# Attention with relative bias and a gated MLP on one core: softmax transposed in 32x32 blocks, and the value product in eight small tiles

## The chip, the core and the metric

The kernel runs on one core of a Trainium2 chip. A core has five engines with a queue each: TensorE (PE, matrix products into PSUM; weight loads are listed apart as PEld), VectorE (DVE), ScalarE (ACT), GpSimd (POOL) and SyncE (SP), which here only issues DMA transfers. The metric is the device time of one execution in microseconds (us); lower is better.

## What is computed

Eight batches, eight heads, 576 positions, head width 64: attention with a bias that a small network makes from the relative position, then a causal five-tap convolution that gates a linear layer, then a second linear layer. All in f32.

```python
scores = scale * np.matmul(q, k.transpose(0, 1, 3, 2))
x = (psi_rel / psi_i)[..., None]
h = np.maximum(x @ w1 + b1, 0.0)
bias = h @ w2
scores = scores + bias.transpose(2, 0, 1)[None, :, :, :]
attn = np.exp(scores - max); attn = attn / (sum + 1e-09)
x = np.matmul(attn, v)                      # then heads side by side: 512 columns
gate_pre += conv_w[k] * xp[:, k:k + S, :]   # k = 0..4
out = (1 / (1 + np.exp(-gate_pre))) * (x @ w_val) @ w_out
```

## The kernel before

**Order.** The Python code does not issue instructions at once. Each step is added to a planner (`Plan.add`) with the engines that may do it, a price on each, the steps it depends on, a priority and the buffers it takes. `Plan.order` simulates the engines with these prices and emits the steps in the order that it finds; on each engine they then run strictly in that order, and wait for one another by semaphores. `OFFS`, `PAIR_AT`, `MLP_AT`, `LOOK` and `LOAD` are tuned numbers of that planner, `BUFS` the number of buffers of each ring: `sp` are score buffers of two PSUM banks, `ps` single PSUM banks, `e` SBUF tiles for exponentials, `pt` tiles for transposed ones.

**Stages.** First the bias for all heads is made in 36 row groups (L338 to L380) and stored to DRAM. Then 32 pairs follow. A pair is one batch `b`, one half of the heads `hg` and one `l`: two heads, stacked on the upper and the lower 64 partitions. `RUNS` gives the order of the pairs; the bias tiles of a half of the heads stay in SBUF during a run and are loaded again at the next (`load_bias`). When all four pairs of a batch are done, its `mlp` may start.

**A pair.** The 576 queries are four chunks of 128 and a last one of 64. For each chunk: scores of both heads (`qkm`, L617), two 64-row tiles of PE side by side; logits with the row minimum (`logits`, DVE, L659); exponential with row sum (`expo`, ACT, L671). For the last 64 queries both heads share one tile, one head above the other, over 640 columns padded with a large negative bias (L629). Then the weights must be transposed so that keys lie on partitions. `TRANS` chooses one of two ways for each pair:
- "T" (13 pairs): the weights are scaled (`norm`, L716), transposed on PE (`tp`, L756) into PSUM, copied out (`tev`), and multiplied with V in f32 (`piece`, L826).
- "D" (19 pairs): the weights are split into two f16 parts (`top`, `rest`, L247, L254), transposed by DMA (`swap`), and multiplied with V, which is split and transposed too (L559 to L575), in three f16 products. The scaling follows at the end: reciprocals are transposed (L876), spread over rows (`rb`, L883) and multiplied in (`mu`, L887).

The last 64 queries have their own value product (`rem_mm`, L902). The result goes straight into the batch's tile `xp` in the batch's second run; in its first run it is stored to DRAM (`store`) and loaded again (`ldx`).

**The MLP.** In seven batches the convolution runs through PSUM in halves of 288 columns (`taps`, L1009 and L1016, all but the first tap on DVE). In the last batch `conv`, `prod` and `acc` do it in SBUF (L966 to L981) on three engines. The products with `w_val` (`val`, L1073) and `w_out` (`outp`, L1130) take three passes each with operands split in two parts.

Of the kernel before, what the change touches and what calls it, by code (L numbers as in the profile page):

```python
# [10 lines left out]
F16 = mybir.dt.float16  # L11
# [21 lines left out]
NEG = -1.0e30  # L33
RW = S + REM
# [4 lines left out]
RUNS = ((0, (0, 1, 2, 3)), (1, (0, 4, 1, 5, 2, 6, 3)), (0, (4, 5, 6, 7)), (1, (7,)))  # L39
MLP_STEPS = 32  # L40
MLP_AT = (28, 16, 18, 8, 12, 10, 17, 38)
PAIR_AT = (-0.5, -1, -2.5, -0.5, -2, 1, 2.5, -2, -2.5, -2.5, 2.5, -1.5, -1.5, -2, 2.5, -1.5, 1.5, -2.5, 0, 2, 1.5, 1.5, -2.5, -0.5, -3.5, -5, -7.5, -7.5, 0, -0.5, 0.5, 1.5)
TRANS = tuple(x == "T" for x in "TTTTDTTTTTTDDTDDDDDTDTDDDDDDDDDD")
BUFS = dict(w=13, d=5, pt=2, sp=2, ps=4, qk=3, rel=4, be=6, xp=2, xh=1, gh=1, gx=1, rt=2)
RING = dict(er="w", hlr="w", raw="w", e="d", hl="d", xo="w", vt="w", ptr="w", gate="w", gf="w", ot="w", tt="ps", po="ps", pm="ps", cv="ps")
LOOK = dict(w=20.89, ps=50.18, d=6.14, be=3.54, gh=38.67, pt=1.31, xh=172.47, sp=0.72, xp=0.18)
DRAIN = 0.07
# [3 lines left out]
    "conv acc relu norm rest top split_hi split_lo glo ghi vlo double_step w_sub w_lo cw".split()  # L51
)
MODES = dict(qkm=1, piece=2, rem_mm=2, bias_mm=3, rb=4)
SMALL = (("G", 0.19), ("V", 0.08))
LOAD = dict(P=0.95, V=1.2, A=0.36, G=0.47, S=0.08)
OFFS = dict(ldx=1, swap=4, qk_ld=1.75, qkm=-5, norm=4, piece=4, val=0.75, outp=7.25, mur=3.25, bias_store=2.5, conv=-1.75, taps=-2.25, split_hi=0.25, rb=-7.5, rest=-9.25, rev=-10, ldv=0.5, w_hi=8, logits=1.75, relu=0, ost=1.25, bias_fin=1.5, ote=-2.5, double_step=5.25, store=4.75, ghi=1, sig=3, vtr=1.25, recip=-4.25, glo=-2.75, ev=-1.5, tev=4.25, evr=3.5, w_sub=-1.75, gf=0.5, w_ld=-1.25, mu=-1, w_lo=7.5, bias_mm=0.5, bias_ld=1.5, expo=0.75, rtp=-0.25, prod=5.25, vlo=3.25, cw=2, vhi=3.25, eps=-2.25, vmax=-6.25, acc=-0.25, split_lo=2, close_bias=1.5, rem_mm=0, top=0.75, vinv=-0.25, tp=-6.25)
# [19 lines left out]
class Plan:  # L76
# [10 lines left out]
    def add(self, engines, fn, deps=(), pri=0.0, takes=(), uses=(), hold=0.5, wire=0.0):  # L87
        pri += OFFS.get(getattr(fn, "func", fn).__name__, 0.0)
        t = Task(engines, fn, [d for d in deps if d is not None], pri, list(takes))
        t.pri = max([pri] + [d.pri for d in t.deps])  # L90
        t.n, t.hold, t.wire = len(self.tasks), hold, wire
        name = getattr(fn, "func", fn).__name__
        t.shares = "GV" if name in SHARED else "G"
        t.mode = MODES.get(name, 0)
        for b in uses:
            b.users.append(t)
        self.tasks.append(t)
        return t

    def order(self):  # L100
# [30 lines left out]
        while ready:  # L131
# [28 lines left out]
            e = min(pick, key=lambda e: pick[e][1])  # L160
# [6 lines left out]
            else:  # L167
                if e == "P":
# [4 lines left out]
                    cost = cost * (2 if slow else 1) + 0.012 + DRAIN * (t.mode != mode)  # L173
# [32 lines left out]
def attention_gated_mlp(  # L206
# [3 lines left out]
    vd: bass.AP,  # L210
    vn: bass.AP,
# [5 lines left out]
    identd: bass.AP,  # L217
    seld: bass.AP,
# [12 lines left out]
    for k in set(BUFS) & {"sp", "ps", "w", "d", "pt", "qk"}:  # L231
# [85 lines left out]
    def bias_rows(m):  # L317
# [10 lines left out]
        pbs = [Buf("tt") for _ in pieces]  # L328
# [20 lines left out]
        for g in range(4):  # L349
            eng = [("A", 0.22 + 0.54 * w / S)] if g == 0 else [("V", 0.1 + 0.4 * w / S), ("G", 0.15 + 2.6 * w / S)]  # L350
# [4 lines left out]
        def bias_mm(e, j):  # L355
            pb = bank(pbs[j])
            x, y = pieces[j]
            for g in range(4):
                T.matmul(
                    pb[32 * g : 32 * g + 32, 0 : y - x],  # L360
# [7 lines left out]
        def bias_fin(e, j, lo, hi, back):  # L368
# [3 lines left out]
            i = pbs[j].t[:, lo - x : hi - x]  # L372
# [10 lines left out]
        first = None  # L383
        for j, (x, y) in enumerate(pieces):
            t = add([("P", 0.1 + 0.5 * (y - x) / HS)], partial(bias_mm, j=j), rts, pri + 0.3, [pbs[j]], [rel[0]])
            for back, n, l in ((False, wf, fs), (True, wb, bs)):
                lo, hi = max(x, 1 if back else 0), min(y, n)
                if lo >= hi:
# [7 lines left out]
                    [pbs[j]],  # L396
# [27 lines left out]
    def load_bias(run, hg, l, c, pri):  # L424
# [3 lines left out]
        def bias_ld(e):  # L428
            if c < NM:
                SP.dma_start(biasm[l][c], bias_rows_of(c, 2 * p, 2))  # L430
            else:
                SP.dma_start(biasr[l][0:REM, 0:S], bias_rows_of(c, 2 * p, 1))
                SP.dma_start(biasr[l][REM:P, REM:RW], bias_rows_of(c, 2 * p + 1, 1))

# [50 lines left out]
    def weight(src, n, hi_lo, k, last, pri):  # L485
        b = {}

        def w_ld(e):
            b["r"] = pools["mp"].tile([P, 1024], I32, name="wraw", tag="xp0")[:, 0 : 2 * n]
# [34 lines left out]
    spilled, arrived, taker = {}, {}, {}  # L524

    def pair(n):
        hg, b, l = order[n]
        p = 2 * hg + l
        run = sum(1 for x in range(1, n + 1) if order[x][0] != order[x - 1][0])
        s0 = PER * n + PAIR_AT[n]  # L530
        tr = TRANS[n % len(TRANS)]
        top_, bot = slice(0, D), slice(D, P)

        qk = Buf("qk")

        def qk_ld(e):
            SP.dma_start(new(qk, [P, S + RW], F32), qkd[b, p])

        loaded = add([("S", 1.73)], qk_ld, (), s0 - 8, [qk])
        vt = Buf("vt")  # L540
        sc = {}
        if tr:

            def ldv(e):
                new(vt, [P, 5, P], F32)
                SP.dma_start(vt.t.rearrange("p t d -> p (t d)"), vn[b, p])

            tv = add([("S", 0.9)], ldv, (), s0 - 1, [vt])
        else:
            vhl, raw = Buf("raw"), Buf("raw")  # L550

            def ldv(e):
                new(vhl, [P, 2, RW], F16)
                new(raw, [P, RW], F32)
                SP.dma_start(raw.t, vd[b, p])

            def vmax(e):
                sc["t"] = smp.tile([P, 4], F32, name="vsc", tag="vsc", bufs=5)
                V.tensor_reduce(out=sc["t"][:, 0:1], in_=raw.t, op=ALU.max, axis=AX.X, apply_absolute_value=True)  # L559

            def vscale(e):
                t = sc["t"]
                (V if e == "V" else G).tensor_scalar(
                    out=t[:, 1:2], in0=t[:, 0:1], scalar1=1e-30, scalar2=2.0**-12, op0=ALU.max, op1=ALU.mult
                )

            def vinv(e):
                t = sc["t"]
                V.reciprocal(out=t[:, 2:3], in_=t[:, 1:2])

            def vhi(e):
                A.activation(out=vhl.t[:, 0, :], in_=raw.t, func=AF.Copy, scale=sc["t"][:, 2:3])

            def vlo(e):
                V.scalar_tensor_tensor(  # L575
# [654 lines left out]
```

## Time and profile before

| | before |
|---|---|
| median of 2 runs | 764.64 us (762.93 to 766.36) |
| span of the profiled execution | 759.0 us |
| instructions | 17283 |
| largest queue | q1: 258420 packets, 133.95 MB |

The page gives the span of the profiled execution, from its first to its last instruction; its own device time isn't listed beside it. The median of the runs is 5.64 us above the span. The busy share of an engine is the time in which at least one of its instructions runs. In a group's row stand line, engine, operation, output<-inputs, shapes and count, then the busy time of the group, the mean of one instruction in ns, and the idle time just before them with what ended it. An f32 matmul leaves two records.

### The profile page before, as it was taken

How to read it: one execution, taken by the hardware profiler on the slowest of the kernel's cores; microseconds unless marked ns; L12 is line 12 of the kernel's file. 1: busy time of each engine (PE TensorE's matmuls, PEld its weight loads, DVE VectorE, ACT ScalarE, POOL GpSimd, SP SyncE). 2: the span in 40 equal slices, each digit the busy share in tenths (PEclk: the TensorE clock that was granted, in tenths of full speed). 3: DMA queues.
4: the chain of work that ended last, by engine and by line, in shares of the span. 5: the costliest groups of instructions: out<-in, count | busy, mean ns of one | idle time of the engine just before them, and what ended most of it. 6: DMA issues, size and time to landing. Idle time of an engine off the chain costs nothing.

```text
span 759.0 us, 17283 instructions
## 1 busy us (share of the span) xinstructions
PE 716.5 (94%) x6091; PEld 485.7 (64%) x6091; DVE 587.5 (77%) x1606; ACT 580.8 (77%) x1302; POOL 476.1 (63%) x550
## 2 busy tenths in 40 slices
PE   5577999999999999999899999999999999999997
PEld 2124666665566666767566677666767786767886
DVE  6996878777789897886759778869998878856830
ACT  6996788767578897889767876789797967797642
POOL 0002467765455685777975494859797587768852
PEclk9999999999999999999999999999999999999999
DMA  8898442968332878899999599599999999999702
GB/s 293 284 287 287 134 119 69 223 198 260 127 111 82 165 157 200 175 196 186 221 207 197 162 243 274 119 221 214 212 175 222 218 265 243 255 193 187 134 29 70
DMA packets 263754, 144.48 MB, mean 190 GB/s; under 512 B 231538, under 2 KB 231796, under 8 KB 263668
## 3 DMA queue, kind: packets, MB, share of 16 engines
q1 hardware_dynamic: 258420, 133.95, 76.7%
q10 hardware_dynamic: 5248, 9.44, 3.9%
q8 instruction: 48, 0.79, 0.4%
q14 instruction: 38, 0.31, 0.1%
HBM read 61.03 MB, written 25.05 MB: 113 GB/s over the span
## 4 chain that ended last, share of the span: by engine, by line
PE 50%; POOL 3%; DMA 3%; DVE 3%; ACT 2%; issue 1%; SPq 0%; POOLq 0%; DVEq 0%; ACTq 0%
PE t_ps L1073 12%; PE t_ps L1130 11%; PE t_sp L617 10%; PE t_ps L826 9%; DMA t_pt<-t_d 3%; PE t_sp L629 2%; PE t_ps L883 2%; PE t_ps L756 2%; POOL t_d L254 2%; PE t_ps L902 2%; PE t_ps L876 1%; DVE t_d L659 1%; ACT t_d L671 1%; DVE xl L254 0%; POOL xl L254 0%
## 5 line engine op out<-in xcount | busy, mean ns | idle before, releaser
L671 ACT ACTIVATE t_d<-t_d,nm 128x576 f32<-128x576 f32 x256 | 197.9, 774 | 67.7 <-DVE nm L659 67.0
L254 POOL TENSOR_TENSOR t_d<-t_d 128x576 f16<-128x576 f32 x152 | 198.1, 1315 | 36.1 <-ACT t_d L247 29.5
L659 DVE CUSTOM_DVE_ANT_0 t_d<-t_sp,bias 128x576 f32<-128x576 f32 x256 | 187.7, 750 | 35.6 <-PE t_sp L617 24.7
L716 POOL TENSOR_SCALAR t_d<-t_d,rinv 128x576 f32<-128x576 f32 x104 | 79.6, 777 | 148.5 <-DVE rinv L698 91.7
L617 PE MATMUL t_sp<-t_qk 64*128 64x288 f32 x1024 | 169.3, 432 | 3.2 <-DVE nm L659 3.1
L826 PE MATMUL t_ps<-t_pt,t_w 128*64 128x256 f16 (+1 forms) x1660 | 140.9, 311 | 4.8 <-DMA t_pt<-t_d 2.5
L617 PEld LDWEIGHTS t_sp<-t_qk 64*128 64x128 f32 x1024 | 95.0, 188 | 52.9 <-issue 13.4
L1016 DVE SCALAR_TENSOR_TENSOR t_ps<-t_xp,convw,t_ps 128x288 f32<-128x288 f32 x168 | 87.2, 519 | 5.6 <-ACT t_ps L1007 2.7
L1073 PE MATMUL t_ps<-xh,wv 128*128 128x320 f32 (+1 forms) x512 | 84.4, 302 | 1.1 <-DVE rt L249 1.1
L1073 PEld LDWEIGHTS t_ps<-xh,wv 128*128 128x128 f32 x512 | 71.9, 188 | 12.4 <-issue 7.3
L247 ACT CAST t_d<-t_d 128x576 f16<-128x576 f32 x113 | 74.6, 668 | 2.9 <-PE t_ps L756 0.4
L1130 PE MATMUL t_ps<-wo,gh 128*128 128x512 f32 x256 | 71.9, 409 | 0.7 <-ACT gh L247 0.6
L826 PEld LDWEIGHTS <-t_w 128*64 128x64 f16 x1140 | 57.4, 109 | 22.2 <-issue 18.9
L756 PE MATMUL t_ps<-identr,t_d 128*128 128x128 f32 x468 | 67.1, 281 | 0.8 <-POOL t_d L716 0.3
L756 PEld LDWEIGHTS t_ps<-identr,t_d 128*128 128x128 f32 x468 | 50.8, 140 | 23.0 <-issue 9.8
L247 ACT COPY t_pt<-t_ps 128x512 f32<-128x512 f32 (+1 forms) x104 | 50.8, 514 | 13.8 <-PE t_ps L756 13.7
L1130 PEld LDWEIGHTS t_ps<-wo,gh 128*128 128x128 f32 x256 | 44.7, 188 | 18.3 <-issue 6.4
L247 ACT COPY t_w<-t_ps 128x512 f32<-128x512 f32 (+2 forms) x65 | 32.6, 501 | 31.2 <-PE t_ps L1130 20.2
L1083 DVE TENSOR_TENSOR t_w<-t_ps,t_w 128x256 f32<-128x256 f32 (+1 forms) x64 | 29.0, 454 | 33.0 <-PE t_ps L1073 26.6
L254 POOL TENSOR_TENSOR gl<-t_w,gh 128x256 fp32r<-128x256 f32 x53 | 40.8, 771 | 16.2 <-PE t_ps L1130 12.8
L826 PEld LDWEIGHTS t_ps<-t_pt,t_w 128*64 128x64 f32 x520 | 33.0, 136 | 28.0 <-issue 10.7
L251 POOL TENSOR_SCALAR t_d<-t_d 128x576 f16<-128x576 f32 x36 | 25.2, 700 | 37.9 <-ACT t_d L671 30.4
(116 smaller groups left out, 1207.4 us busy)
## 6 DMA issues: line engine op xcount, KB each, us to landing
t_qk<-qkd SPq DMA_DIRECT2D x32, 608.0 KB, 4.7
bias<-bias_d SPq DMA_DIRECT2D x32, 576.0 KB, 5.1
bias_d<-t_be SPq DMA_DIRECT2D x36, 295.5 KB, 4.7
out<-t_w ACTq DMA_DIRECT2D x32, 256.0 KB, 3.2
t_w<-vd SPq DMA_DIRECT2D x19, 320.0 KB, 3.5
xs<-t_w SPq DMA_DIRECT2D x16, 288.0 KB, 3.6
t_xp<-xs SPq DMA_DIRECT2D x8, 576.0 KB, 4.7
t_w<-vn SPq DMA_DIRECT2D x13, 320.0 KB, 5.1
```

The lines of the kernel that those rows point to most:

```text
L247: A.copy(out=out, in_=in_)
L254: (V if e == "V" else G).tensor_tensor(out=out, in0=in0, in1=in1, op=ALU.subtract)
L617: T.matmul(ts[a][:, j, 0:hw], lhsT=q_[r, c * P : (c + 1) * P], rhs=k_[r, a * REM + j * hw : a * REM + (j + 1) * hw], start=True, stop=True,)
L659: V.tensor_tensor_reduce(out=part().rearrange("p (j f) -> p j f", j=2), in0=sp.t[:, :, 0 : w // 2], in1=bias.rearrange("p (j f) -> p j f", ...
L671: A.activation(out=part(), in_=part(), func=AF.Exp, bias=nms[c][:, a : a + 1], scale=-1.0, accum_out=sums[c][:, a, 0:1],)
L716: (G if e == "G" else V).tensor_scalar(out=t, in0=t, scalar1=rinvs[c][:, a : a + 1], scalar2=1.0, op0=ALU.mult, op1=ALU.mult,)
L756: T.transpose(t[:, k * P : (k + 1) * P], es[c].t[:, (k0 + k) * P : (k0 + k + 1) * P], ident)
L826: T.matmul(po.t[r, 0:256], lhsT=vt.t[:, v0 + t, r], rhs=pt[:, w, :, :] if tr else pt[:, :, w, :], start=(k == 0), stop=(k == 5 * len(prods ...
L1016: V.scalar_tensor_tensor(out=o, in0=x, scalar=cw, in1=t, op0=ALU.mult, op1=ALU.add)
L1073: T.matmul(pm.t[:, 0:w], lhsT=pools["wv"][wi][:, k, d * P : (d + 1) * P], rhs=xb.t[xi][:, k, 0:w], start=(q == 0 and k == 0), stop=(q == 2 ...
L1083: V.tensor_tensor(out=gf_.t[:, 0:w], in0=pm.t[:, 0:w], in1=gates[d].t[:, t0 : t0 + w], op=ALU.mult)
L1130: T.matmul(pm.t, lhsT=gb.t[gi][:, k, o : o + P] if o < 256 else gx.t[gi][:, k, :], rhs=pools["wo"][wi][:, k, :], start=(q == 0 and k == 0) ...
```

## The change

One way takes the place of the two. Softmax weights are scaled (`norm`) and then transposed by DVE within 32x32 blocks (`turn_`): afterwards partition 32i + k holds key 32j + k of the queries of block i, for each key block j. The value product (`av`) therefore contracts over 32 keys at a time: for each of 18 key blocks, four row groups of 32 partitions and two heads (64 columns each), in f32, 128 or 160 columns of queries at a time. V is laid out by the host in 32-row blocks and repeated for the four row groups (`vr`). The scores of the last 64 queries of two consecutive pairs are computed together (`qkr`) in four 64x64 tiles, without padding. Identity, DMA transposes, f16 parts, late scaling and the trip of x through DRAM are gone. The runs now take the batches in turn, nine runs in place of four, and every batch's convolution works as the last one's did, with one block in four by fused taps and three by products and sums. The `pt` ring has one buffer, `sp` three, `ps` two. The planner's tuned numbers differ throughout, the bias stage uses `sp` buffers, and its `relu` may run on ACT as well.

```diff
-RUNS = ((0, (0, 1, 2, 3)), (1, (0, 4, 1, 5, 2, 6, 3)), (0, (4, 5, 6, 7)), (1, (7,)))
+RUNS = ((0, (0,)), (1, (0, 1)), (0, (1, 2)), (1, (2, 3)), (0, (3, 4)), (1, (4, 5)), (0, (5, 6)), (1, (6, 7)), (0, (7,)))
...
-BUFS = dict(w=13, d=5, pt=2, sp=2, ps=4, qk=3, rel=4, be=6, xp=2, xh=1, gh=1, gx=1, rt=2)
+BUFS = dict(w=10, d=5, pt=1, vx=2, sp=3, ps=2, qk=2, rel=4, be=6, xp=2, xh=1, gh=1, gx=1)
...
-DRAIN = 0.07
+DRAIN = (0.18, 0.21, 0.16, 0.16, 0.16)
...
-LOAD = dict(P=0.95, V=1.2, A=0.36, G=0.47, S=0.08)
+LOAD = dict(P=2, V=1.98, A=0.95, G=0.67, S=1.21)
...
+        nr = [add([("G", 0.73), ("V", 0.43)], partial(norm, a=a), [t], h + heads + 0.6 + a / 2) for a in range(heads)]
...
+        def ldv(e):
+            new(vx, [P, NJ, P], F32)
+            SP.dma_start(vx.t.rearrange("p j d -> p (j d)"), vr[b, p])
...
+                def qkr(e, sps=sps):
+                    ts = [new(sp, [P, 2, 512], F32) for sp in sps]
+                    for j in range(2):
+                        for y, q_ in enumerate((qk, qk2)):
+                            for a, r in enumerate((top_, bot)):
+                                x = (j + a) % 2
+                                T.matmul(
+                                    ts[y][(top_, bot)[(a + y) % 2], x, 0:HS],
+                                    lhsT=q_.t[r, NM * P : S],
+                                    rhs=q_.t[r, S + x * HS : S + (x + 1) * HS],
+                                    start=True,
+                                    stop=True,
+                                )
...
+            def turn_(e, c=c, eb=eb, first=first):
+                if first is None:
+                    new(xt, [P, 2 * NM + 1, S], F32)
+                if c < NM:
+                    V.transpose(out=xt.t[:, c : 9 - c : 8 - 2 * c, :], in_=eb.t.rearrange("p (a f) -> p a f", a=2))
                 else:
...
+                    V.transpose(out=xt.t[:, NM, :], in_=eb.t)
...
+            pv = xt.t.rearrange("p s (j q) -> p s j q", q=32)
+            for j in range(j0, j0 + NJ // 3):
+                for i in range(4):
+                    for a in range(2):
+                        k = NM + (i // 2 == (a + l) % 2)
+                        r, o = slice(32 * i, 32 * i + 32), (top_, bot)[a]
+                        T.matmul(
+                            avs[i // 2].t[o, i % 2, 0 : 32 * k],
+                            lhsT=vx.t[r, j, o],
+                            rhs=pv[r, 0:k, j, :] if a == 0 else pv[r, 8 : 8 - k : -1, j, :],
+                            start=j == 0,
+                            stop=j == NJ - 1,
                         )
...
+        for j0 in range(0, NJ, NJ // 3):
+            u = [xt, vx] if j0 == 2 * NJ // 3 else ()
+            ta = add([("P", 1.53)], partial(av, j0=j0), turned + [tv, ta], s0 + 13, () if ta else avs, u)
...
+            copy(
+                e,
+                x[:, 0 : NM * P].rearrange("p (c i q) -> p i c q", c=NM, i=4)[:, 2 * h : 2 * h + 2],
+                t[:, :, 0:P].rearrange("p i (c q) -> p i c q", c=NM),
             )
...
+            copy(e, x[r, NM * P : S].rearrange("p (i q) -> p i q", i=2), t[r, :, P : P + 32])
...
-        for k in range(NK) if final else ():
+        for k in range(NK):
...
-                elif k >= 2:
+                elif k >= 1:
                     y = add([("A", 0.67), ("G", 0.75)], prod, d[:1], x - 0.2, [tmp], [xp])
-                    convs[k] = add([("V", 0.67), ("G", 1.3)], acc, [convs[k], y], x, (), [tmp])
+                    convs[k] = add([("V", 0.67), ("G", 1.45)], acc, [convs[k], y], x, (), [tmp])
```

`logits`, `expo`, the row sums, the score matmuls of the four chunks, and the products `val` and `outp` compute what they did.

More of the change, by code (lines that the diff above doesn't have):

```diff
@@ L598, in pair @@
-        halves = [Buf("pt"), Buf("pt")]
-        ptr = Buf("ptr")
-        nms, rinvs, sm, invs, rsum = {}, {}, None, {}, {}
-        es, exps, inv = {}, {}, {}
-        moved = {}
-        sums = {}
-        hls = {}
-        for c in range(NM + 1):
-            w = S if c < NM else RW
-            sps = [Buf("sp") for _ in range(2 if c < NM else 1)]
-            def qkm(e, c=c, sps=sps):
-                q_, k_ = qk.t[:, 0:S], qk.t[:, S : S + RW]
-                ts = [new(sp, [P, 2, 512], F32) for sp in sps]
-                if c < NM:
-                    hw = S // 2
+        qk, loaded = load_qk(n)
@@ new lines, in pair, with qkm @@
+        vx = Buf("vx")
+        def ldv(e):
+            new(vx, [P, NJ, P], F32)
+            SP.dma_start(vx.t.rearrange("p j d -> p (j d)"), vr[b, p])
+        tv = add([("S", 3.3)], ldv, (), s0 - 2, [vx])
+        xt, first, turned = Buf("pt"), None, []
+        for c in range(NM + 1):
+            h = s0 + 2 * c
+            if c < NM:
+                sps = [Buf("sp") for _ in range(2)]
+                def qkm(e, c=c, sps=sps):
+                    ts = [new(sp, [P, 2, 512], F32) for sp in sps]
@@ L941, in attention_gated_mlp @@
+        t = None
+        for h in range(2):
+            new_ = b not in taker
+            d = [ta, t] + ([] if t else ([closed] if b == order[0][1] else [wdone]) if new_ else [taker[b]])
+            t = add([("A", 0.45), ("V", 0.5)], partial(ev, h=h), d, s0 + 13.5, [xo] if new_ else (), [avs[h]])
+            taker.setdefault(b, t)
+        ready.setdefault(b, {})[p] = t
     left = []
@@ L949, in mlp @@
         xp, convs = arrived[b], {}
-        y0 = 2 * next(x for x, z, _ in order if z == b)
-        def ldx(e):
-            SP.dma_start(xp.t[:, y0 : y0 + 2, 4 : 4 + S], xs[b][y0 : y0 + 2].rearrange("k p t -> p k t"))
-        ld = add([("S", 1.65)], ldx, [spilled[b][y0], spilled[b][y0 + 1], taker[b]], st)
-        lds = [ld if k // 2 == y0 // 2 else spilled[b][k] for k in range(NK)]
-        i, prev = 0, None
-        for k in range(NK) if final else ():
+        lds = ready[b]
+        i = 0
+        for k in range(NK):
             for tp in range(TAPS):
```

548 lines of the change are left out of this document (131 added, 417 removed).

## The prediction

> **What bounds the kernel now.** I read the busy shares first, then the chain of work that ended last, then the busy times of three stretches, then PE by groups and in order of time, and DVE last.
>
> ```profile
> span 759.0 us, 17283 instructions
> PE 716.5 (94%) x6091; PEld 485.7 (64%) x6091; DVE 587.5 (77%) x1606; ACT 580.8 (77%) x1302; POOL 476.1 (63%) x550
> ...
> PE 50%; POOL 3%; DMA 3%; DVE 3%; ACT 2%; issue 1%; SPq 0%; POOLq 0%; DVEq 0%; ACTq 0%
> ```
>
> ```profile
> core 0: us, PE busy (x) PEld busy (x) DVE busy (x) ACT busy (x) POOL busy (x), PEclk, DMA share, GB/s
> 0.00:80.00 80.00, 54.47 (x486) 22.75 (x487) 64.32 (x171) 62.82 (x135) 8.83 (x34) 0.96 0.84 278
> 80.00:720.00 640.00, 628.12 (x5396) 434.56 (x5393) 515.36 (x1421) 505.60 (x1141) 451.86 (x497) 1.00 0.85 188
> 720.00:759.00 39.00, 33.95 (x213) 28.39 (x212) 7.86 (x15) 12.37 (x27) 15.40 (x21) 0.99 0.14 48
> ```
>
> Between 80 and 720 us PE is busy for 628.1 of 640 us (98%) at full granted clock; it is the bound, and in the chain no other engine has over 3%. The first 80 us build the bias (DVE 64.3, ACT 62.8, DMA share 0.84); the last 39 us are the last batch's gated MLP, with 7.9 us on DVE. I keep both ends and rebuild the middle. The page gives no time for the profiled execution beside its span of 759.0; the median of the two runs lies 764.64 - 759.0 = 5.6 above it, and I add that 5.6 at the end.
>
> **PE: what goes and what comes.**
>
> ```profile
> L826 PE MATMUL t_ps<-t_pt,t_w 128*64 128x256 f16 (+1 forms) x1660 | 140.9, 311 | 4.8 <-DMA t_pt<-t_d 2.5 <-ACT t_pt L247 1.7 <-ACT xh L247 0.6
> L756 PE MATMUL t_ps<-identr,t_d 128*128 128x128 f32 x468 | 67.1, 281 | 0.8 <-POOL t_d L716 0.3 <-ACT t_pt L247 0.2
> ...
> L629 PE MATMUL t_sp<-t_qk 64*64 64x320 f32 x256 | 41.4, 442 | 4.7 <-DVE nm L659 4.6
> ...
> L883 PE MATMUL t_ps<-rt,sel 2*128 2x256 f32 x76 | 26.4, 426 | 0.3 <-ACT t_w L855 0.3
> L902 PE MATMUL t_ps<-t_w 128*64 128x64 f16 (+1 forms) x830 | 23.0, 207 | 0.0
> ```
>
> ```profile
> 304.26 1.24 PE L617 MATMUL t_sp<-t_qk 64*128 64x288 f32 x8
> 305.43 0.77 PE L756 MATMUL t_ps<-identr,t_w 128*128 128x128 f32 x5
> 306.13 2.38 PE L826 MATMUL t_ps<-t_pt,t_w 128*64 128x256 f32 x20
> 308.44 0.38 PE L876 MATMUL t_ps<-identr,rinvs 128*2 128x128 f32 x2
> ```
>
> ```profile
> 459.95 1.29 PE L629 MATMUL t_sp<-t_qk 64*64 64x320 f32 x8
> 461.17 1.50 PE L826 MATMUL t_ps<-t_pt,t_w 128*64 128x256 f16 x24
> ```
>
> The value product, the transposes, the row broadcast of the reciprocals, the value product of the last 64 queries and the old last-query scores all go: 140.9 + 67.1 + 26.4 + 23.0 + 41.4 = 299. Group times count edges twice (the 2.38 us group is followed 2.31 us later), by 3 to 10%; three small groups that go too (transposes from t_w, L876, L912) hold about as much, so 299 stands.
>
> ```profile
> L359 PE MATMUL t_ps<-rel,w 128*32 128x512 f32 x16 | 2.1, 598 | 1.2 <-ACT t_be L378 1.2
> ```
>
> New value product (`av`): 18 key blocks x 4 row groups x 2 heads = 144 small f32 matmuls a pair, two records each (512 score matmuls give the 1024 records of L617). Price per streamed column: the f32 group of 20 records is ten passes of 256 columns, two column tiles side by side, in 2.31 us, 0.90 ns a column; 0.90 x 288 x 4 = 1.04 gives the score group's 1.17 (304.26 to 305.43) with 0.13 for the change of tile form. With eight tiles side by side a key block costs 2 x 160 x 0.90 = 0.29 us, a pair 18 x 0.29 = 5.2, 32 pairs 166. The trace shows two row tiles (L617) and two column tiles (L826) at once, and in the bias stage four column tiles: 16 records of 512 columns at 0.90 would be 7.4 us one by one and take 2.1, 3.5 at once. Eight is what the form of the change asks, and its four row groups write to four different banks. If only four run at once: 10.4 a pair, 333 in all. I take 5.2, since rows and columns each pack without loss in these rows.
>
> Joint last queries: two pairs share one group of four 64x64 tiles, 1.04 + 0.13 = 1.17 for two, where each took 1.22 (459.95 to 461.17): 16 x 1.17 = 19 added; two tiles at a time, twice that. The score matmuls and both MLP products stay. PE after: 716.5 - 299 + 166 + 19 = 602.
>
> **DVE: what goes and what comes.**
>
> ```profile
> L1016 DVE SCALAR_TENSOR_TENSOR t_ps<-t_xp,convw,t_ps 128x288 f32<-128x288 f32 x168 | 87.2, 519 | 5.6 <-ACT t_ps L1007 2.7
> L1016 DVE SCALAR_TENSOR_TENSOR t_w<-t_xp,convw,t_ps 128x288 f32<-128x288 f32 x56 | 28.8, 515 | 2.3
> ...
> L575 DVE SCALAR_TENSOR_TENSOR t_w<-t_w,vsc 128x640 f16<-128x640 f32 x19 | 20.7, 1090 | 0.5 <-ACT t_w L572 0.5
> ...
> L559 DVE TENSOR_REDUCE vsc<-t_w 128x1 f32<-128x640 f32 x19 | 15.4, 810 | 2.5 <-DMA t_w<-vd 2.5
> L249 DVE COPY t_pt<-t_ps 128x512 f32<-128x512 f32 x22 | 15.0, 682 | 0.2
> ...
> L887 DVE TENSOR_TENSOR t_xp<-t_xp,t_ps 128x256 f32<-128x256 f32 x24 | 10.0, 418 | 4.8 <-ACT t_xp L855 4.7
> L1009 DVE TENSOR_SCALAR t_ps<-t_xp,convw 128x288 f32<-128x288 f32 x17 | 8.7, 514 | 1.2 <-DMA t_xp<-xs 1.2
> L249 DVE COPY t_pt<-t_ps 128x128 f32<-128x128 f32 x30 | 8.6, 286 | 3.6 <-PE t_ps L756 3.5
> ...
> L887 DVE TENSOR_TENSOR t_w<-t_w,t_ps 128x256 f32<-128x256 f32 x14 | 5.9, 418 | 3.2 <-ACT t_w L855 3.1
> ```
>
> ```profile
> 458.64 0.75 DVE L659 CUSTOM_DVE_ANT_0 t_d<-t_sp,bias 128x576 f32<-128x576 f32 x1
> ...
> 459.32 0.75 DVE L659 CUSTOM_DVE_ANT_0 t_d<-t_sp,bias 128x576 f32<-128x576 f32 x1
> ```
>
> ```profile
> L966 DVE SCALAR_TENSOR_TENSOR t_w<-t_xp,convw,t_w x8: 819/1514/1987, 703.2 to 714.8; 128x576 f32<-128x576 f32 x8
> ```
>
> Off DVE: the convolution through PSUM of seven batches (87.2 + 28.8 + 8.7), the split of V (20.7 + 15.4), evictions of transposes (15.0 + 8.6) and the late scaling (10.0 + 5.9): 200. Smaller groups that go (the 2x256 copies, 64-wide scalings) and smaller ones that come (38 more row sums and reciprocals, DVE's share of the new evictions) are set against each other.
>
> On DVE, the turns (`turn_`): 4 of 1152 elements and 1 of 576 a pair. No row shows a DVE transpose. Logits of 576 elements follow each other after 0.68 us (458.64 to 459.32); the copies of 512 and 128 elements (0.682 and 0.286) give 1.03 ns for each further element. So 0.68 + 576 x 1.03 = 1.27 for 1152, 0.68 for 576: 5.76 a pair, 184 in all. I take it as the operation has one input and no reduction. Bounds: the 1152 without any fixed cost, 1.03 ns each, 1.19 (172 in all with 0.59); and the slowest row per element, L575 with two inputs, 1.70 ns, 1.96 and 0.98 (282 in all).
>
> Convolution: seven more batches work as the last one did: one block in four with four fused taps on DVE (7 x 4 = 28 operations, 0.82 to 1.99 each by the L966 row; I take 1.44, below its median, 40 in all, bounds 23 and 56), the other three with 84 products on ACT or POOL and 84 adds on DVE or POOL. With both inputs in SBUF the L966 operation goes from 0.82 to 1.99 us for one size, beside a busy POOL; I price an add at 1.3 and give DVE a third of them (the planner's weight for DVE is three times POOL's): 36. None is 0, half 55. DVE after: 587.5 - 200 + 184 + 40 + 36 = 647.
>
> **ACT, POOL, queues.**
>
> ```profile
> L671 ACT ACTIVATE t_d<-t_d,nm 128x576 f32<-128x576 f32 x256 | 197.9, 774 | 67.7 <-DVE nm L659 67.0
> L247 ACT CAST t_d<-t_d 128x576 f16<-128x576 f32 x113 | 74.6, 668 | 2.9 <-PE t_ps L756 0.4 <-DMA t_pt<-t_d 0.3 <-POOL t_d L254 0.3
> L247 ACT COPY t_pt<-t_ps 128x512 f32<-128x512 f32 (+1 forms) x104 | 50.8, 514 | 13.8 <-PE t_ps L756 13.7
> ```
>
> ```profile
> L254 POOL TENSOR_TENSOR t_d<-t_d 128x576 f16<-128x576 f32 x152 | 198.1, 1315 | 36.1 <-ACT t_d L247 29.5 <-DVE nm L659 2.4 <-PE t_ps L756 0.6
> L716 POOL TENSOR_SCALAR t_d<-t_d,rinv 128x576 f32<-128x576 f32 x104 | 79.6, 777 | 148.5 <-DVE rinv L698 91.7 <-PE t_ps L756 14.9 <-issue 7.9
> ...
> L981 POOL TENSOR_TENSOR t_w<-t_w 128x576 f32<-128x576 f32 x8 | 12.3, 1541 | 1.4 <-ACT t_w L976 0.9
> ```
>
> ```profile
> DMA packets 263754, 144.48 MB, mean 190 GB/s; under 512 B 231538, under 2 KB 231796, under 8 KB 263668
> ```
>
> ACT: 580.8 - 74.6 - 50.8 + at most 64 x 2 x 0.51 for the new evictions + 84 x 0.77 for products = 586 at most. POOL: 476.1 - 198.1 + 184 more scalings (288 less 104) x 0.78 + 56 adds x 1.54 = 508. Both stay under DVE. SP: every DMA transpose (and with them most of the 231538 packets under 512 B) and the stores and reloads of x go; it gains V four times over (32 x 1.18 MB by its size in the code) and bias reloads for nine runs instead of four (72 of 0.59 MB). By the sizes in the code some 130 MB, below the 144.5 of now, so SP costs nothing in the middle; the first 80 us move 278 GB/s at a share of 0.84, and 2.6 MB more of V there would be up to 9 us. I take 0: the first score waits for the bias stage, which DVE and ACT fill.
>
> New waits: a turn waits for its scaling on POOL, and a pair's first turn also for the last value product of the pair before (`pt=1`). Behind a waiting turn on DVE stand the next logits, which free the score banks PE needs. That is the third rival.
>
> **The sum.** Ends kept: 80 + 39 us, with 64.3 + 7.9 of DVE's work. The middle then holds 647 - 72 = 575 us of DVE. PE reached 98% beside engines with slack; DVE will stand beside a PE at (602 - 88) / 593 = 87%, so 97%: 593 us. 593 + 119 + 5.6 = 717 us, 6% below 764.64. Its own range: without adds and with the short fused taps DVE has 594, (594 - 72) / 0.98 + 125 = 657; with half the adds, a middle at 95%: 647 + 19 = 666, 625 + 125 = 750.
>
> **The rivals.**
> 1. Slower, PE stays the bound: only four of the eight tiles run at once. PE 602 + 167 = 769, (769 - 88) / 0.98 + 125 = 820. Between, it decides where PE holds (764.6 - 125) x 0.98 + 88 = 715, an `av` of 8.7 us a pair. For it: no row shows more than four tiles, and none four row tiles. Against: both directions pack nearly without loss in the rows.
> 2. Slower, DVE over-full: a turn pays the price of a small operation for every 128 columns, nine times the 0.286 of the 128-element copy, 2.57 us. That is 128 x 1.30 + 32 x 0.61 = 186 more, DVE 833, (833 - 72) / 0.97 + 125 = 910. It decides from 45 more than 647, a turn of 1.6 us. Against it: in the row for 512 elements the fixed part is paid once. The Trainium skill, "VectorE: DVE Perf Modes", "The three transpose paths", has 311 ns for 128 columns; nine of these would be 2.80 us and the sum by it 944. "Vector Engine (DVE) Microarchitecture Reference", 3.8, has one element per cycle and lane, which is the other reading; no run shown yet decides.
> 3. No change: single buffers couple PE and DVE. `av` takes two of the three score buffers for 5.2 us and its evictions, some 5.8, in which no logits can come. The middle gives a pair about 593 / 31 = 19.1 us (an estimate: the first pair falls before it); 13.3 remain for 9 x 0.68 + 5.76 = 11.9 us of logits and turns. If that fails by 1.5 us a pair, 46 us are lost: 763. Against it: five `e` buffers let turns wait and MLP work fill DVE meanwhile.
>
> **How the numbers follow.** Forecast 717 with 0.65 (657 to 749); below 657 with 0.02; third rival 0.18, of it 0.02 slower; first 0.10; second 0.05. About 2% is what a measurement here can tell from no change, 749 to 780. Faster 0.67, same 0.16, slower 0.17. The range, 672 to 778, leaves out the two slow rivals and a little below.
>
> **What would show it.** A turn at 1.2 to 1.4 us; an `av` third (6 key blocks, 96 records) near 1.7 us; DVE above 85% and PE below 86% of the span; no DMA transpose. Wrong if the chain still has PE at half with `av` over 8 us a pair, if turns pass 1.6 us, or if DVE idles on scalings and `av`.

## The result, and the profile after

The kernel after the change takes 826.60 us (median of 2 runs, 821.82 to 831.37) against 764.64: 1.081 times as long, 95% interval 1.073 to 1.089. The forecast was 717, and DVE as the bound. The first lines are from the page of the kernel after; they answer to the page lines, the PE groups and the DVE groups of before.

```profile
span 829.4 us, 28463 instructions
...
PE 693.3 (84%) x12056; PEld 495.1 (60%) x12056; DVE 562.4 (68%) x1363; ACT 482.3 (58%) x1089; POOL 539.3 (65%) x678
...
PEclk9997668776799999999999999999989999999999
...
DMA packets 44254, 131.15 MB, mean 158 GB/s; under 512 B 4704, under 2 KB 4832, under 8 KB 40032
...
q8 instruction: 94, 1.54, 0.8%
...
L644 DVE STREAM_TRANSPOSE t_pt<-t_d 128x1152 f32<-128x1152 f32 x128 | 171.6, 1363 | 136.3 <-PE t_sp L665 129.9
L665 PE MATMUL t_sp<-t_pt,t_vx 32*64 32x160 f32 (+1 forms) x9216 | 203.4, 311 | 62.6 <-issue 54.3
...
L606 PE MATMUL t_sp<-t_qk 64*128 64x288 f32 x1024 | 197.2, 462 | 48.2 <-DVE nm L540 32.1
...
L736 POOL TENSOR_TENSOR t_w<-t_w 128x576 f32<-128x576 f32 x96 | 136.7, 1424 | 7.8 <-ACT t_w L731 4.4
...
L341 PE MATMUL t_sp<-rel,w 128*32 128x288 f32 (+17 forms) x352 | 46.5, 537 | 11.9 <-ACT rel L319 4.0
```

DVE has 85 us less than forecast and PE 91 us more. L665 is `av`, L644 the long turn, L606 the scores. In front of `av` stand 54.3 us of "issue": PE idle with nothing that the profile shows to wait for. The queue q8, on which instructions arrive, carries 94 packets of 16.4 kB (1.54 MB / 94); before it carried 48:

```profile
q8 instruction: 48, 0.79, 0.4%
```

The busy times of three stretches of the kernel after (columns as in the prediction: PE, PEld, DVE, ACT, POOL, granted clock, DMA share, GB/s):

```profile
75.00:245.00 170.00, 126.69 (x2081) 88.90 (x2082) 134.81 (x322) 86.95 (x199) 112.34 (x120) 0.74 0.46 152
245.00:720.00 475.00, 421.01 (x8051) 313.50 (x8057) 324.11 (x792) 282.89 (x661) 345.82 (x440) 0.98 0.49 161
720.00:829.40 109.40, 91.56 (x1532) 74.04 (x1532) 45.68 (x107) 53.54 (x114) 67.29 (x92) 0.98 0.20 68
...
790.40:829.40 39.00, 33.43 (x189) 28.31 (x180) 4.64 (x11) 11.02 (x20) 21.92 (x34) 0.99 0.14 48
```

There are two different stories, and an end of 39 us that is the old one. From 75 to 245 us PE has holes and its clock falls to 0.74, while DVE is the busiest engine (79%). From 245 us on DVE is at 68% and PE at 89%, with most of its holes inside `av`. PE in order of time, two value products late in the kernel after:

```profile
719.26 4.61 PE L665 MATMUL t_sp<-t_pt,t_vx 32*64 32x160 f32 x137 [1.52 <-issue]
724.20 2.42 PE L665 MATMUL t_sp<-t_pt,t_vx 32*64 32x128 f32 x128 [0.33 <-issue]
727.67 0.77 PE L665 MATMUL t_sp<-t_pt,t_vx 32*64 32x128 f32 x23 [1.05 <-issue]
744.13 0.50 PE L665 MATMUL t_sp<-t_pt,t_vx 32*64 32x128 f32 x8 [1.94 <-issue]
744.79 2.42 PE L665 MATMUL t_sp<-t_pt,t_vx 32*64 32x160 f32 x127 [0.17 <-DVE nm L540]
747.88 2.42 PE L665 MATMUL t_sp<-t_pt,t_vx 32*64 32x160 f32 x128 [0.67 <-issue]
751.35 0.77 PE L665 MATMUL t_sp<-t_pt,t_vx 32*64 32x160 f32 x25 [1.05 <-issue]
```

After a first stretch that varies, the matmuls come in bursts of 128, each with its weight load: 256 instructions, and 16.4 kB / 256 is 64 bytes for one. A burst takes 2.42 us, 0.30 us per key block (16 records), close to the 0.29 of the prediction. But the next one starts 3.47 us after it (724.20 to 727.67, 747.88 to 751.35); over the twelve bursts of 126 to 128 records in the trace the step is 3.1 to 4.0 us. One `av` thus lasts 744.13 to 752.12, 8.0 us, and not 5.2. The packets of q8 show the same step: in the trace of the kernel after no two of the 94 start less than 3.3 us apart and 37 follow within 4.1, while in the kernel before no two of the 48 start less than 11.0 us apart. Transfers of data are not what delays `av`; the busy share of the DMA engines from 720 to 760 us, a digit for each us, is 0 from 740 to 753 but for one slice at a tenth:

```profile
DMA  9978300008798048579200000100000008995000
```

The chain that ended last says little here: it could be followed back over 15% of the span only.

```profile
PE 6%; DVE 3%; issue 2%; POOL 2%; ACT 2%; DVEq 0%; POOLq 0%
```

### The profile page after: what moved, and what is told of

Same layout as the page of the kernel before. It is cut to its first block, busy times and chain, and to the rows that moved or that the text cites. A ratio compares the mean times of both kernels' runs of the same rounds, so it can differ in the third digit from the quotient of the medians.

```text
span 829.4 us, 28463 instructions
## 1 busy us (share of the span) xinstructions
PE 693.3 (84%) x12056; PEld 495.1 (60%) x12056; DVE 562.4 (68%) x1363; ACT 482.3 (58%) x1089; POOL 539.3 (65%) x678
## 3 DMA queue, kind: packets, MB, share of 16 engines
q8 instruction: 94, 1.54, 0.8%
## 5 line engine op out<-in xcount | busy, mean ns | idle before, releaser
L644 DVE STREAM_TRANSPOSE t_pt<-t_d 128x1152 f32<-128x1152 f32 x128 | 171.6, 1363 | 136.3 <-PE t_sp L665 129.9
L665 PE MATMUL t_sp<-t_pt,t_vx 32*64 32x160 f32 (+1 forms) x9216 | 203.4, 311 | 62.6 <-issue 54.3
L566 POOL TENSOR_SCALAR t_d<-t_d,rinv 128x576 f32<-128x576 f32 x256 | 197.5, 787 | 86.9 <-DVE rinv L562 60.6
L553 ACT ACTIVATE t_d<-t_d,nm 128x576 f32<-128x576 f32 x256 | 197.2, 771 | 96.4 <-DVE nm L540 80.3
L606 PE MATMUL t_sp<-t_qk 64*128 64x288 f32 x1024 | 197.2, 462 | 48.2 <-DVE nm L540 32.1
L665 PEld LDWEIGHTS t_sp<-t_pt,t_vx 32*64 32x64 f32 x9216 | 177.5, 140 | 90.4 <-issue 69.2
L606 PEld LDWEIGHTS t_sp<-t_qk 64*128 64x128 f32 x1024 | 109.4, 199 | 115.4 <-DVE nm L540 58.3
L736 POOL TENSOR_TENSOR t_w<-t_w 128x576 f32<-128x576 f32 x96 | 136.7, 1424 | 7.8 <-ACT t_w L731 4.4
L240 ACT COPY xp<-t_sp 128x256 f32<-128x256 f32 x126 | 32.0, 289 | 148.0 <-PE t_sp L665 147.0
L796 PE MATMUL t_ps<-xh,wv 128*128 128x320 f32 (+1 forms) x512 | 87.1, 307 | 2.6 <-DVE t_w L806 1.8
L796 PEld LDWEIGHTS t_ps<-xh,wv 128*128 128x128 f32 x512 | 72.9, 192 | 20.8 <-issue 12.7
L341 PE MATMUL t_sp<-rel,w 128*32 128x288 f32 (+17 forms) x352 | 46.5, 537 | 11.9 <-ACT rel L319 4.0
L247 POOL TENSOR_TENSOR xl<-xp,xh 128x256 fp32r<-128x256 f32 (+1 forms) x64 | 50.7, 812 | 0.1
L553 ACT ACTIVATION_READ_ACCUMULATOR t_d<-t_d,nm 128x1 f32 x256 | 47.9, 187 | 0.0
L731 ACT ACTIVATE t_w<-xp,convw 128x576 f32<-128x576 f32 x61 | 44.8, 765 | 4.6 <-POOL t_w L736 3.0
L796 PE MATMUL t_ps<-xl,wv 128*128 128x256 f32 (+1 forms) x256 | 46.7, 304 | 0.0
```

The costliest lines, as they stand in the source:

```text
L247: (V if e == "V" else G).tensor_tensor(out=out, in0=in0, in1=in1, op=ALU.subtract)
L341: T.matmul(pb.t[32 * g : 32 * g + 32, j, 0 : y - x], lhsT=w28, rhs=rel[g].t[:, x:y], start=True, stop=True, tile_position=(0, 32 * g),)
L553: A.activation(out=x, in_=x, func=AF.Exp, bias=st["nm"][:, a : a + 1], scale=-1.0, accum_out=st["sm"][:, a, 0:1])
L566: (G if e == "G" else V).tensor_scalar(out=t, in0=t, scalar1=st["r"][:, a : a + 1], scalar2=1.0, op0=ALU.mult, op1=ALU.mult)
L606: T.matmul(ts[a][:, j, 0:HS], lhsT=qk.t[r, c * P : (c + 1) * P], rhs=qk.t[r, S + j * HS : S + (j + 1) * HS], start=True, stop=True,)
L644: V.transpose(out=xt.t[:, c : 9 - c : 8 - 2 * c, :], in_=eb.t.rearrange("p (a f) -> p a f", a=2))
```

## The experiments

The theories: **A**, PE's instructions are not supplied fast enough in `av`; **B**, the single `pt` buffer and the three score buffers couple PE and DVE (the prediction's third rival); **C**, the low clock between 75 and 225 us costs the time; **D**, the gaps come from the 32-row form; **E**, DVE binds that early stretch. Ratios are to the kernel before, with 95% intervals.

| run | us | ratio |
|---|---|---|
| half_count | 760.56 | 0.996 (0.993 to 0.999) |
| same_count | 819.52 | 1.072 (1.065 to 1.078) |
| half_columns | 833.15 | 1.093 (1.087 to 1.099) |
| two_xt | 810.36 | 1.064 (1.059 to 1.069) |
| one_xt_small | 817.88 | 1.073 (1.066 to 1.079) |
| half_two_xt | 757.08 | 0.990 (0.987 to 0.993) |
| warm | 814.32 | 1.063 (1.057 to 1.070) |
| no_split | 815.91 | 1.066 (1.063 to 1.070) |
| half_early | 749.01 | 0.981 (0.977 to 0.985) |
| half_both | 728.04 | 0.952 (0.947 to 0.957) |
| spread | 841.06 | 1.101 (1.096 to 1.106) |
| spread_warm | 841.06 | 1.102 (1.097 to 1.107) |

The 826.60 us of the kernel after are the median of two runs 9.5 us apart, and same_count, one_xt_small, warm and no_split all lie 7 to 12 us below it. Differences of this size from 826.60 therefore say little by themselves.

**Half of the instructions (half_count), and the same number in another form (same_count).**

```diff
-                for i in range(4):
+                for i in range(2):
...
-                        r, o = slice(32 * i, 32 * i + 32), (top_, bot)[a]
+                        r, o = slice(64 * i, 64 * i + 64), (top_, bot)[a]
...
-                            avs[i // 2].t[o, i % 2, 0 : 32 * k],
+                            avs[i].t[o, j % 2, 0 : 32 * k],
```

For same_count each of these 64-column tiles is split into two of 32 columns.

> The value product with four tiles of 64 rows and 64 columns in place of eight of 32 rows and 64 columns: 144 matmuls for a pair instead of 288, the same 5.2 us of streamed columns, the order of all instructions unchanged. It adds query blocks of different rows together, so the value product is not the reference's. Theory A (the bursts of exactly 128 matmuls with about 1 us of idle time called issue between them are the supply of PE's instructions): the idle time called issue in front of the value product falls from 54 us to under 15, one value product takes under 6 us, and the time falls from 826.6 by 40 to 90 us. Theory B (the single buffer of turned softmax and the three score buffers set the pace, PE's gaps are only where it shows): the time moves by less than 15 us. Theory D (the gaps come from the form with 32 rows): the same gain as A, so this run alone does not part A and D.

> The value product with eight tiles of 64 rows and 32 columns: 288 matmuls for a pair as after the change, but no tile of 32 rows; the columns streamed in each tile stay 128 or 160, so the ideal time stays 5.2 us. It also adds query blocks of different rows together, so the value product is not the reference's. Theory A (number of instructions): the bursts of 128 matmuls and the gaps of about 1 us stay, 45 to 60 us of issue in front of the value product, the time within 15 us of 826.6. Theory D (the form with 32 rows): the gaps go, the time is that of the run with 144 matmuls.

The instructions, the queue q8 and the group of the value product on the page of half_count, then that group on the page of same_count:

```profile
span 758.6 us, 19247 instructions
...
q8 instruction: 58, 0.95, 0.5%
...
L665 PE MATMUL t_sp<-t_pt,t_vx 64*64 64x128 f32 (+1 forms) x4608 | 185.7, 307 | 14.0 <-issue 6.7
```

```profile
L667 PE MATMUL t_sp<-t_pt,t_vx 64*32 64x128 f32 (+1 forms) x9216 | 195.9, 302 | 62.0 <-issue 54.1
```

With half of the instructions 54.3 us of issue become 6.7, `av` costs 200 us with its idle time (185.7 + 14.0) after 266 (203.4 + 62.6), and the kernel is 66 us faster. There are 9216 instructions fewer (28463 to 19247) and 36 packets fewer on q8 (94 to 58), 256 for each packet: q8 carries PE's instructions. With the full number in tiles of 64 rows 54.1 us of issue stay. The number of instructions decides, not the form; D falls.

**Half of the columns, all of the instructions (half_columns).**

```diff
+                        w = 32 if j == 0 else 16
...
-                            avs[i // 2].t[o, i % 2, 0 : 32 * k],
+                            avs[i // 2].t[o, i % 2, 0 : w * k],
...
-                            rhs=pv[r, 0:k, j, :] if a == 0 else pv[r, 8 : 8 - k : -1, j, :],
+                            rhs=pv[r, 0:k, j, 0:w] if a == 0 else pv[r, 8 : 8 - k : -1, j, 0:w],
```

> The value product with the tiles, instructions and order of the kernel after the change, but all key blocks after the first stream half of their columns (64 or 80 instead of 128 or 160); half of the value product is left out. Streaming would take 2.7 us a pair instead of 5.2. Theory A (PE's instructions arrive at about 73 a microsecond, 576 for a pair, so 7.3 to 8 us a pair whatever they stream): the time stays within 15 us of 826.6, and the idle time called issue in front of the value product grows from 54 us to 100 us or more. If the streamed columns set the pace, one value product falls to about 5 us and the time falls by 50 us or more.

Its value-product group and clock from the page, then PE in order of time at the place of the 724.20 row above:

```profile
PEclk9997665575887998999988998999899899888899
...
L666 PE MATMUL t_sp<-t_pt,t_vx 32*64 32x80 f32 (+3 forms) x9216 | 149.4, 263 | 88.0 <-issue 82.3
```

```profile
723.38 1.67 PE L666 MATMUL t_sp<-t_pt,t_vx 32*64 32x64 f32 x128 [1.21 <-issue]
726.85 0.80 PE L666 MATMUL t_sp<-t_pt,t_vx 32*64 32x64 f32 x23 [1.80 <-issue]
```

The burst shrinks from 2.42 to 1.67 us, the gap behind it grows from 1.05 to 1.80, and the next burst still starts 3.47 us later, behind the same records (128, then 23). The step between bursts is that of 256 instructions, whatever they stream. Nearly half of the product's columns are gone, and the whole kernel gains nothing: it takes 6.6 us longer. That total holds two effects. `av` with its idle time falls from 266 to 237 us (149.4 + 88.0), where 2.5 us less for each of the 32 pairs would have made it 186. The rest of PE pays it back (the scores take 212.0 us after 197.2) at a mean granted clock of 0.858 after 0.930, which fits PE's longer holes but was not shown to come from them. The issue time grew to 82.3, not to the 100 that I expected as the least. The Trainium skill, "Runtime: NRT & Kernel Launch", "Instruction fetch mechanics", says that instructions arrive in blocks of 16 KiB, 256 of them, which these bursts and packets bear out; it also calls the cost of crossing a block "mostly hidden", and here the trace differs: about 1 us a block.

**Two buffers for the turned weights (two_xt, its control one_xt_small, half_two_xt).** The lines of two_xt:

```diff
-        pools["wv"] = [mp.tile([P, NK, DM], F32R, name=f"wv{i}") for i in range(2)]
+        pools["wv"] = [mp.tile([P, NK, DM], F32R, name="wv")] * 2
...
-                    new(xt, [P, 2 * NM + 1, S], F32)
+                    xt.t = pools["pt"].tile([P, 2 * NM + 1, S], F32, name="t_pt", tag=f"pt{n % 2}")
```

> Two buffers for the turned softmax in place of one, taken in turn by pairs, the order of all instructions unchanged. To make room the high and the low part of the weights share a buffer, and V is loaded in 13 of its 18 key blocks, the others read again from these, so the output is not the reference's. Theory B (one buffer couples the engines): DVE's 130 us of waiting for the value product in front of its turns fall below 30 us and the time falls by 40 us or more. Theory A (PE's instruction supply sets the steady pace, the wait of DVE is slack): the wait of DVE falls as well or moves to the scores, but the time falls by less than 20 us, since PE was already 97 per cent occupied from 245 to 785 us.

> Control for the run with two buffers: the same weights' buffer and the same shortened V, but one buffer for the turned softmax as in the kernel after the change. All theories: within 10 us of 826.6; what it differs by is what the shared weight buffer and the smaller load of V do, and the run with two buffers is compared with this one.

> The 144 matmuls a pair of the run before and two buffers for the turned softmax together (again V in 13 of 18 key blocks and a shared buffer for the two parts of the weights; the output is not the reference's). With one buffer the run with 144 matmuls takes 760.6 us, and two buffers beside 288 matmuls brought 8 us. If the single buffer binds once the instruction supply does not (theory B in a weaker form), the time falls from 760 by more than 15 us, and DVE's 62 us of waiting for the value product go. If PE is then the bound by its own work from 245 us on (671 of 759 us busy), the time is within 10 us of 752.

The long turn on the page of two_xt, then of its control:

```profile
L644 DVE STREAM_TRANSPOSE t_pt<-t_d 128x1152 f32<-128x1152 f32 x128 | 171.3, 1360 | 11.1 <-POOL t_d L566 10.8
```

```profile
L644 DVE STREAM_TRANSPOSE t_pt<-t_d 128x1152 f32<-128x1152 f32 x128 | 171.6, 1363 | 126.4 <-PE t_sp L665 119.8
```

The second buffer takes away all of DVE's 120 us of waiting for `av`, and the time moves by 8 us against the control, with intervals that overlap; without the supply gaps it is 3.5 us (760.56 to 757.08), there without a control of its own. This is DVE's largest wait on the page after the change, and nearly all of it was slack: DVE waited for an engine that was late anyway. B in its strong form falls.

**The early stretch (warm, no_split, half_early).** warm puts this behind the score matmuls of the first six pairs; no_split leaves out six of DVE's eight splitting operations (`double`) on each weight part (of the three steps kept, the first only takes its tiles); half_early joins both to half_count:

```diff
+                    if n < 6:
+                        warm = pools["ps"].tile([P, 512], F32, name="warm", tag="ps0")
+                        for j in range(2):
+                            r = top_
+                            T.matmul(
+                                warm[:, 0:HS],
+                                lhsT=qk.t[r, 0:P],
+                                rhs=qk.t[r, S : S + HS],
+                                start=True,
+                                stop=True,
+                            )
...
-        double(b, b["r"], n)[i](e)
+        if i in (0, 4, 5):
+            double(b, b["r"], n)[i](e)
```

> Behind the score matmuls of the first six pairs two more matmuls of 288 columns go to a bank that nobody reads (24 times about 1.2 us of PE at full clock, 29 us in all, between 60 and 205 us); nothing else changes. Theory C (the half clock costs the early phase its time): the granted clock between 80 and 215 us rises from 0.7 to over 0.9, the score matmuls' total falls from 197 us towards 172, and the time falls by 10 to 30 us. Theory E (DVE binds there): the clock may rise, but the time stays within 6 us of 826.

> Of DVE's eight steps on a 512-wide part of the weights (nine parts, about 42 us between 80 and 209 us) only two are left, so the weights are not the reference's; nothing else changes. Theory E (the early phase is bound by DVE, and the products of the weights start only when these steps are done): about 32 us of DVE go, the weights are ready 20 to 30 us earlier, and the time falls by 15 to 32 us. Theory C (PE's half clock from 75 to 225 us is what makes the early pairs slow, DVE only waits along): less than 10 us.

> Three losses taken away together: 144 matmuls a pair (760.6 us alone), the fillers of the first six pairs (12 us alone) and two of eight splitting steps of the weights (11 us alone); the output is not the reference's. If the three are independent: 733 to 741 us. If fillers and splitting steps remove the same wait of the early phase twice: 745 to 752 us. Below 725 would mean that they help each other, and that the prediction's 717 us missed nothing else.

The score matmuls of the kernel after, grouped from 80 to 240 us, then from 245 to 700 us:

```profile
L606 PE MATMUL t_sp<-t_qk 64*128 64x288 f32 x222 | 58.9, 569 | 33.3 <-DVE nm L540 18.8 <-ACT xp L240 10.0 <-DVE rinv L562 2.9
```

```profile
L606 PE MATMUL t_sp<-t_qk 64*128 64x288 f32 x656 | 112.4, 432 | 5.7 <-DVE nm L540 4.5 <-DVE rinv L562 0.9
```

The same instruction takes 569 ns early and 432 later, as long as in the whole of the kernel before. From 75 to 245 us PE is granted 0.74 of its clock, while it waits for DVE's row minima above all. The Trainium skill, "TensorE: Matmul & The Clock Gate", "Part 1: The HAM clock gate (the "warmup" mystery)", has half clock after an idle window of about 3.4 us; the trace agrees where the idle time is long: behind the 9.96 us without work before 207.75 us (its row stands in the section on why the prediction was wrong) the granted clock from 207 to 213 us is 0.50. The busy times from 80 to 215 us, first of the kernel after, then of warm, then of no_split:

```profile
80.00:215.00 135.00, 98.57 (x1669) 68.86 (x1666) 113.13 (x263) 67.91 (x154) 85.99 (x89) 0.70 0.51 168
```

```profile
80.00:215.00 135.00, 103.37 (x1758) 74.09 (x1758) 115.28 (x266) 68.40 (x155) 86.51 (x90) 0.81 0.50 169
```

```profile
80.00:215.00 135.00, 101.91 (x1718) 71.50 (x1718) 88.08 (x223) 71.75 (x164) 88.83 (x95) 0.73 0.49 165
```

The fillers raised the clock from 0.70 to 0.81, not to the 0.9 of the expectation, the scores' total fell by 2 us only (197.2 to 195.4 us), and 12 us were gained on the median. no_split took 25 us off DVE in this stretch, to 65% busy, but the first product with the weights came only 8 us earlier (202.51 us in place of 210.82), and 11 us were gained, between what E and C expected. So E falls in its strong form: the amount of DVE's work alone is not what this stretch waits for. Both gains are little more than the 9 us by which the control one_xt_small differs from the kernel after. Together, without the supply gaps, they bring 12 us (760.56 to 749.01) and not 23, which fits that they remove the same time twice. The fillers in the groups of PE in half_early:

```profile
L615 PE MATMUL warm<-t_qk 64*128 64x288 f32 x96 | 31.6, 456 | 0.0
```

**PE relieved further (half_both):** both cuts, 144 matmuls and half of the columns.

> 144 matmuls a pair and half of the columns in all key blocks after the first two: 288 instructions and 2.7 us of streaming a pair; the output is not the reference's. It relieves PE beyond the 760.6 us of the run with 144 matmuls. If PE's own work is the bound from 245 us on, the time falls by 25 to 65 us (1.3 us a pair if the supply then binds at 73 a microsecond, 2.5 us if the columns do, over 25 pairs) to 695 to 735. If DVE binds next, as the prediction had it (its 562 us and the ends of 119 us put it at about 700), the time stops near there; if the single buffers bind, it stays above 750.

Its busy times, the same columns as above:

```profile
245.00:700.00 455.00, 421.95 (x5517) 310.04 (x5510) 357.25 (x874) 324.25 (x751) 393.21 (x497) 0.97 0.53 175
```

The time is 728 us, 11 above the forecast although `av` streams little more than half, and even there PE is busy for 93% of the stretch (96% in half_count, 437 of 455 us) and DVE for 79%. The part of `av` that was cut still lay on the path, so PE is the bound from 245 us on in half_count and in this run; DVE is not reached.

**Another order (spread, spread_warm).** The planner is told of the supply and puts other matmuls between the thirds of `av`; spread_warm adds the fillers:

```diff
+                    if t.mode == 3:
+                        z = max(s, f)
+                        w = z + max(0.0, (NEED - min(CAP, credit + (z - stamp) * RATE)) / RATE)
+                        if w > s:
+                            s = w
```

> The same work as after the change, in an order that the kernel's own planner makes once it is told of the supply: a third of the value product (192 of PE's instructions) may start only when a store of 200, refilled at 73 a microsecond (256 in 3.5 us, as the fetches stand in the trace), holds 192, so that products of the weights or scores are put between the thirds. Theory A: the idle time called issue in front of the value product falls from 54 us below 25. The time: if all that idle time was loss on the path, 826.6 falls by 25 to 50 us; if the other order loses as much elsewhere (scores held longer, turns waiting), it stays within 10 us. The planner itself puts this order at 832 us.

> The order of the run before with the 24 small fillers behind the score matmuls of the first six pairs. If the fillers' 12 us and the order's gain are independent, the time is 10 to 14 us below the run with the order alone.

```profile
PE 718.5 (86%) x12056; PEld 507.4 (60%) x12056; DVE 560.0 (67%) x1357; ACT 478.8 (57%) x1076; POOL 547.2 (65%) x697
...
L615 PE MATMUL t_sp<-t_qk 64*128 64x288 f32 x1024 | 213.1, 480 | 58.6 <-DVE nm L549 40.1
...
L674 PE MATMUL t_sp<-t_pt,t_vx 32*64 32x128 f32 (+1 forms) x9216 | 208.6, 314 | 30.9 <-issue 18.2
```

On the page of spread the issue time falls from 54.3 to 18.2 us, as A says, but the time grows by 14, outside both expected ranges: PE's busy time rises by 25 us and its waits for row minima from 32.1 to 40.1. What was saved in the gaps was paid again by the other order; which part of it pays was not separated. The fillers bring nothing on top, against the expectation, which is a second reason not to credit the 12 us of warm to the clock. Of the runs that leave nothing out (warm, spread, spread_warm) none is faster than the kernel before.

## Why the prediction was wrong

**The step that failed** is in the sum: "The middle then holds 647 - 72 = 575 us of DVE ... so 97%: 593 us". DVE was never the bound after 245 us. PE was, because the term "a pair 18 x 0.29 = 5.2, 32 pairs 166" counted streamed columns only. The column price held, 0.30 us per key block within a burst. What the sum left out is a limit in instructions: 288 records with their weight loads are 576 instructions, 2.25 blocks of 256, by an estimate at 3.47 us each 7.8 us a pair (less where the first block is there already). `av` cost 203.4 us busy and 62.6 us of idle time before its matmuls, 266 instead of 166. Removing the surplus instructions gave 66 of the 110 us between forecast and result.

**The first rival named the right engine with the wrong mechanism.** It put PE as the bound, from "an `av` of 8.7 us a pair" on, at 764.6. All eight tiles do run at once, and one `av` near 8 us already gave 826.6, because the threshold took the rest of PE's work at 602 - 166 = 436 us. That rest measured 490 us (693.3 - 203.4). With it and the 266 of `av` the rival's own formula gives (756 - 88) / 0.98 + 125 = 807 us, an estimate; what is left to 826.6 was not assigned. In the kernel before the scores and the bias matmuls (two groups of the rest) had

```profile
L617 PE MATMUL t_sp<-t_qk 64*128 64x288 f32 x1024 | 169.3, 432 | 3.2 <-DVE nm L659 3.1
...
L359 PE MATMUL t_ps<-rel,w 128*32 128x288 f32 (+17 forms) x352 | 34.4, 500 | 15.4 <-ACT t_be L378 12.7 <-DVE t_be L380 1.4 <-ACT rel L338 1.2
```

and now 197.2 and 46.5: the same counts. For the scores the lower clock of the early stretch is the cause seen above; for the bias matmuls the cause is open.

**"Ends kept: 80 + 39 us"** was half right. The last 39 us are alike. The start is not 80 us long but reaches to about 215: the products with the weights begin at 210.82 us (the first L796 row below), and before that only five `av` run.

```profile
207.75 2.28 PE L606 MATMUL t_sp<-t_qk 64*128 64x288 f32 x6 [9.96 <-ACT xp L240]
210.82 1.22 PE L796 MATMUL t_ps<-xh,wv 128*128 128x256 f32 x4 [0.78 <-POOL xh L244]
```

The kernel before, from 80 to 240 us:

```profile
80.00:240.00 160.00, 157.33 (x1336) 100.66 (x1333) 131.27 (x414) 119.54 (x286) 95.47 (x109) 1.00 0.53 151
```

It kept PE busy for 157 of 160 us, at full clock, in part with the transposes and value products that the change takes away; taking them off PE there left holes and a low clock. The order differs as well. By 240 us the kernel before had run 359 of the 1024 records of the scores and no product with the weights (its first stands at 256.10 us); the kernel after had run 250, and 56 records of products with the weights. Now that the batches come in turn, the weights are asked for earlier.

What this stretch waits for as a whole was not shown. For the longest hole, the 9.96 us above, the trace and the code show a chain. The eight 512-wide parts of the weights are loaded one at a time into a raw buffer that shares its place with a batch's `xp` (the code's tag `xp1`), the first at 84.0 us and the last at 197.6; the planner puts the first eviction of the second batch behind all of them; and that eviction (ACT L240 at 207.22 us) starts behind DVE's last read of the raw buffer (L458, 206.73 to 207.15 us). no_split shortened this chain's DVE steps and moved the first product by 8 us. No run changed the chain itself or the order of the batches, so what they cost in all is open. The last 32 us (749 to 717) lie where PE, not DVE, binds: half_early's PE has 673.4 us, less 31.6 of fillers 642, where the sum had 602. How much of that is clock and how much PE's holes before 245 us stays open as well.

**The third rival** (buffers, 763) described a real wait, 130 us of it, but two_xt shows it to be worth about 8 us beside the gaps, and half_two_xt 3.5 without them.

**What was right:** a turn of 1.36 us (1.27 forecast; the second rival falls), 131 MB of DMA (130), SP nearly without cost (PE waits for DMA for 1.7 us in all), no DMA transposes. On DVE too much was put: all 96 adds ran on POOL, where 36 us were put on DVE; the splits `xl` and `gl`, 28 us on DVE before, moved to POOL too; and a fused tap took 0.92 us where 1.44 was taken. So DVE has 562 us, not 647. The sign that I named for it, an `av` third "near 1.7 us", would have stood inside a burst and still missed the gap between two bursts.

## What to carry to other kernels

Price a packed stream of small matmuls twice, by columns and by instructions (each matmul with its weight load, f32 doubled), and take the larger; here a lasting stream got 256 instructions in 3.47 us, so a tile scheme that multiplies their number by two loses what packing wins. A wait of 130 us on the page says nothing of the time to be gained: give the waiting engine what it waits for in one run before building on it. And work taken off the bound engine pays only in stretches where that engine was the bound: ask for each stretch who is next.

## What the runs showed of the hardware

In a lasting stream of small matmuls, blocks of 128 with their loads follow each other at about 3.5 us (3.1 to 4.0 in the kernel after, 3.2 to 4.0 with half of the columns) whether they stream for 2.42 or 1.67 us, even where no data moves by DMA. Eight tiles of 32x64 stream side by side at 18.9 ns a record in a burst with 128 or 160 columns, 0.30 us a key block where the price per column gives 0.29; tiles of 64x32 at 18.8 (2.41 us for 128 records). With half of the columns it is 13.0 ns and not half of 18.9, at a granted clock of 0.78 around that burst. Breaking such a stream up with other matmuls removed two thirds of the gaps (54.3 to 18.2 us of issue) and still lengthened the kernel by 14 us.
